# Carrying a hand-written instruction order two chunks into the second token block of a fused attention, feed-forward and routed-expert kernel

## The chip, the cores and the metric

The kernel runs on one core of a Trainium2 chip. The metric is the device time of one execution in microseconds (us); the median of three runs of the kernel before is 526.39 us (526.16 to 527.29). TensorE is called PE, VectorE DVE, ScalarE ACT, GpSimd POOL, and SyncE, which issues most of the loads, SP.

## What is computed

Three layers in a row, all in float32. The first is attention with a narrow local window plus one summary key per 32 positions (the maximum of the keys, the mean of the values):

```python
k_sum = k.reshape(B, H, nb, block, D).max(axis=3)
v_sum = v.reshape(B, H, nb, block, D).mean(axis=3)
scores_l = scale * np.matmul(q, k.transpose(0, 1, 3, 2))
...
scores_all = np.concatenate([scores_l_m, scores_s], axis=-1)
scores_all = scores_all - np.max(scores_all, axis=-1, keepdims=True)
a = np.exp(scores_all)
a = a / (np.sum(a, axis=-1, keepdims=True) + 1e-09)
```

with B=2, H=8, S=768, D=64. The second is a feed-forward layer on 1536 tokens of 512 values, with 2048 hidden units and an ELU between its two products. The third routes each token to one of 8 experts by the argmax of a gate, and each expert is a two-product ReLU layer (512 to 1024 to 512) whose result is scaled by two gate factors.

## The kernel before

The tokens go in four blocks, numbered 0 to 3, of 512, 256, 384 and 384 tokens (`UNITS` counts units of 64 tokens: 8, 4, 6, 6). Units 0 to 11 belong to the first batch entry, 12 to 23 to the second. For a unit u the attention runs scores (PE, line 330), maximum (DVE, line 340), exponential (ACT, line 353), normalising (DVE or POOL, line 401), transposing (PE, line 412), copying out of PSUM (ACT, line 419), product with the values (PE, line 449), and the split of the result into a high and a low part, xh (ACT, line 455) and xl (DVE, line 462), which are the inputs of the feed-forward layer. From block 1 on two units are a pair and share PSUM banks S and T.

The feed-forward layer goes through 16 chunks c of 128 hidden units for each block j. Below, h(j,c) is the first product (line 482, twelve matmuls, three for each of four slices, since each operand is a high and a low part), U its two exponent functions on ACT (line 495), V the two DVE steps that finish the ELU (lines 502 and 508; the second reads h out of PSUM and thereby frees its bank), g the split of the result (ACT line 518, DVE line 524), w the split of the second weight (ACT line 175, DVE line 179), and y(j,c) the second product (line 543). h has two PSUM banks, so h(j,c) cannot start before V of the chunk two earlier is done. During block 0 the weights are also unpacked and split (lines 130 to 167), which happens once. When y of a block is complete, it is copied out (lines 555 and 557), stored, transposed and turned into the gate's logits (line 579 on).

The summary keys and values of the second batch entry are reduced on DVE from loads of their own: eight reductions of keys, K (line 227), and eight of values, F (line 239). The copy of the F results into another layout, `pad`, is four DMAs on SP (`vsums2`, line 246), and three DVE copies take it into the value tiles (`v_pad`, line 255). Units 12 and 13 need the K results for their scores and `pad` for their product.

The order up to the transition from block 0 to block 1 is written out by hand in the table `START` of some 620 entries: `start_up` (line 717) walks it, and every engine gets its instructions in that order. An entry is a letter for the step and the numbers of unit, or chunk: `s9` scores of unit 9, `Gf` h of chunk 15, `Yd` y of chunk 13, `o`, `h`, `l` the product, xh and xl. Behind `START` a loop over (block, chunk) takes over, in which only PE has a written order, and a list scheduler at build time places the instructions of the other engines. In before, the loop begins at h(1,0), with y(0,14) and y(0,15) still to do. Each engine executes its instructions in the order in which they were built.

Routing constants (`route_consts`, line 758) are one load of 202 KB and some 14 small POOL instructions. In before they belong to the loop's part, and the scheduler puts them where it finds room.

Of the kernel before, what the change touches and what calls it, by code (L numbers as in the profile page):

```python
# [13 lines left out]
U32 = mybir.dt.uint32  # L14
# [8 lines left out]
E, F2 = 8, 1024  # L23
# [17 lines left out]
QS = (0, 2, 6, 8)  # L41
C3 = 2
WARM = 56
BITS = (0, 1, 2, 3, 6, 8)
PAIRS = {12: 35, 14: 45, 16: 54, 18: 65, 20: 74, 22: 83}
AT = (2, 6, 8, 8)
LQ = 5
# [34 lines left out]
class Prog:  # L82
# [42 lines left out]
    def conv_r(self, c, part):  # L125
# [13 lines left out]
    def conv_t(self, c, part):  # L139
# [112 lines left out]
    def v_pad(self, u):  # L252
# [363 lines left out]
    def part1(self):  # L616
# [22 lines left out]
        steps = [(j, c) for j in range(NBLK) for c in range(NF)]  # L639
        todo = {}  # L640

        def at(hs, fn, *args):
            todo.setdefault(hs, []).append((fn, args))

        for j in range(2, NBLK):
            for n in range(UNITS[j]):
                u = U0[j] + n
                h0 = PAIRS[u - n % 2]
# [28 lines left out]
        h0 = 2 * NF * (NBLK - 1)  # L677
# [39 lines left out]
    def start_up(self):  # L717

        unit = dict(k=self.k_sum, s=self.scores, m=self.maxes, b=self.less_max, e=self.weights, z=self.sums, r=self.recip, R=self.recip2, n=self.norm, t=self.turn_of, c=self.turned,
                    o=self.weighted, h=self.x_hi, l=self.x_lo, p=self.v_pad, x=self.max_k0, w=self.window, a=self.add_eps, M=self.mean_v0, P=self.pad_v0, K=self.red_sum, F=self.mean_v1, Z=self.keep_warm)  # L720
        load = dict(k=self.load_k0, Q=self.load_q0, V=self.load_v0, W=self.load_kw, c=self.load_c, w=self.load_w, q=self.load_q, v=self.load_v, s=self.load_sum, u=self.load_v1)
        part = dict(A=self.conv_r, B=self.conv_t, C=self.conv_f, D=self.conv_h, E=self.conv_l)
        chunk = dict(U=self.elu_act, V=self.elu_dve, Y=self.mm_y, g=self.g_high, f=self.g_low, i=self.w_high, j=self.w_low)
        half = set()
        for u in range(NV):
            self.unit0(u)
        with self.tc.manual_schedule():
            for op in START.split():
# [838 lines left out]
```

## Time and profile before

| what | value |
|---|---|
| median of 3 runs | 526.39 us |
| the profiled execution's own time | 526.98 us |
| its span, first to last instruction | 525.2 us |
| PE busy | 511.6 us (97%) |
| DVE busy | 337.1 us (64%) |
| ACT busy | 305.1 us (58%) |
| POOL busy | 54.4 us (10%) |

The busy shares are averages over very different stages: the attention of block 0 (to about 41 us), the rest of block 0 (to about 126 us), blocks 1 to 3, and the experts. PE's busy time counts modelled ends of matmuls, so gaps between matmul starts say more than the share does.

### The profile page before, as it was taken

The numbers are of one execution on the slowest core, as the hardware profiler recorded it, in microseconds if no ns is written. First come the engines' busy times: TensorE is split into PE (matmuls) and PEld (weight loads), VectorE is DVE, ScalarE is ACT, GpSimd is POOL, SyncE is SP. The second block draws the span as 40 slices with busy tenths as digits, with TensorE's granted clock in tenths as the row PEclk, the third lists the DMA queues.
The fourth block names the chain that finished last, engine by engine and source line by source line (L and its number), as shares of the span: only waits on it lengthen the run. The fifth ranks groups of instructions, "written<-read, shape, count | busy, mean of one in ns | idle before, by whom it ended". The sixth has DMA issues, their size and how long they took to land. (4 is left out here: it accounts for less than half of the span.)

```text
span 525.2 us, 9833 instructions
## 1 busy us (share of the span) xinstructions
PE 511.6 (97%) x3325; PEld 409.6 (78%) x3325; DVE 337.1 (64%) x945; ACT 305.1 (58%) x715; POOL 54.4 (10%) x102
## 2 busy tenths in 40 slices
PE   9999999998999999999999999999999999999994
PEld 6486778886888889888898897987888567576883
DVE  5899999997688868676557899668321011535410
ACT  3899998994677658656546547543232223656421
POOL 3530000001000000000000000113411111100001
PEclk9999999999999999999999999999999999999998
DMA  8999334551311212200001025310689898594601
GB/s 293 405 396 331 119 118 140 179 195 50 132 32 52 81 45 78 82 0 16 2 0 62 1 75 192 96 61 1 183 319 302 297 360 317 174 344 149 203 22 43
DMA packets 37131, 78.08 MB, mean 149 GB/s; under 512 B 3951, under 2 KB 9807, under 8 KB 37072
## 3 DMA queue, kind: packets, MB, share of 16 engines
q1 hardware_dynamic: 34752, 70.02, 39.2%
q0 software_dynamic: 2320, 7.34, 4.0%
q8 instruction: 28, 0.46, 0.4%
q14 instruction: 31, 0.25, 0.2%
HBM read 100.37 MB, written 6.55 MB: 204 GB/s over the span
## 5 line engine op out<-in xcount | busy, mean ns | idle before, releaser
L482 PE MATMUL h<-xh,wi 128*128 128x384 f32 (+2 forms) x528 | 142.8, 338 | 2.5 <-DVE elp L508 1.5
L543 PE MATMUL y<-wsp,gh 128*128 128x512 f32 x368 | 117.3, 400 | 0.0
L482 PEld LDWEIGHTS h<-xh,wi 128*128 128x128 f32 x528 | 94.5, 190 | 10.7 <-DVE elp L508 2.4
L482 PE MATMUL h<-xl,wi 128*128 128x384 f32 (+2 forms) x264 | 87.9, 333 | 1.6 <-DVE xl L462 1.6
L543 PEld LDWEIGHTS y<-wsp,gh 128*128 128x128 f32 x368 | 66.8, 190 | 12.3 <-issue 0.5
L543 PE MATMUL y<-wsp,gl 128*128 128x512 f32 x184 | 72.5, 394 | 0.0
L1222 DVE TENSOR_TENSOR holdl<-S,holdh 128x512 fp32r<-128x512 f32 x22 | 15.2, 690 | 72.5 <-ACT holdh L1218 53.7
L1190 PE MATMUL h<-w2s,holdh 128*128 128x512 f32 x176 | 59.8, 400 | 0.0
L1233 PE MATMUL y<-w2s,holdh 128*128 128x512 f32 x176 | 59.0, 398 | 0.0
L482 PEld LDWEIGHTS h<-xl,wi 128*128 128x128 f32 x264 | 50.2, 190 | 5.6 <-DVE xl L462 1.8
L502 DVE SCALAR_TENSOR_TENSOR elt<-ele,elt 128x384 f32<-128x384 f32 (+2 forms) x64 | 35.5, 554 | 24.6 <-ACT ele L495 24.3
L495 ACT ACTIVATE elt<-h 128x384 f32<-128x384 f32 (+2 forms) x64 | 31.2, 487 | 31.1 <-PE h L482 30.5
L175 ACT CAST wsp<-wo 128x512 fp32r<-128x512 f32 x62 | 38.0, 617 | 16.8 <-PE y L543 16.0
L179 DVE TENSOR_TENSOR wsp<-wo,wsp 128x512 fp32r<-128x512 f32 x62 | 42.6, 689 | 6.3 <-ACT wsp L175 6.0
L518 ACT CAST gh<-elp 128x384 fp32r<-128x384 f32 (+2 forms) x62 | 31.5, 508 | 23.5 <-DVE elp L508 12.8
L524 DVE TENSOR_TENSOR gl<-elp,gh 128x384 fp32r<-128x384 f32 (+2 forms) x62 | 34.0, 549 | 12.2 <-ACT gh L518 11.9
L543 PEld LDWEIGHTS y<-wsp,gl 128*128 128x128 f32 x184 | 34.7, 188 | 8.0 <-DVE gl L524 0.3
L353 ACT ACTIVATE e<-e,nb 128x120 f32<-128x120 f32 x88 | 33.6, 385 | 10.8 <-DVE nb L340 10.8
L1233 PEld LDWEIGHTS y<-w2s,holdh 128*128 128x128 f32 x176 | 33.1, 188 | 8.4 <-issue 1.6
L1190 PEld LDWEIGHTS h<-w2s,holdh 128*128 128x128 f32 x176 | 33.1, 188 | 8.2 <-ACT w2s L1258 0.8
L1264 DVE TENSOR_TENSOR w2s<-wo,w2s 128x512 fp32r<-128x512 f32 x48 | 30.8, 687 | 9.3 <-ACT w2s L1258 7.8
L508 DVE SCALAR_TENSOR_TENSOR elp<-elt,h 128x384 f32<-128x384 f32 (+2 forms) x64 | 35.1, 548 | 0.9
(290 smaller groups left out, 819.8 us busy)
## 6 DMA issues: line engine op xcount, KB each, us to landing
wo<-in_w SPq DMA_DIRECT2D x9, 2048.0 KB
wo<-in_w SPq DMA_DIRECT2D x18, 1024.0 KB
ri<-in_w_in SPq DMA_DIRECT2D x16, 512.0 KB
ro<-in_w_out SPq DMA_DIRECT2D x16, 512.0 KB
wo<-in_w SPq DMA_DIRECT2D x32, 256.0 KB
w2p<-in_w SPq DMA_DIRECT2D x32, 256.0 KB
w2q<-in_w SPq DMA_DIRECT2D x24, 256.0 KB
k<-in_kw SPq DMA_DIRECT2D x18, 192.0 KB
```

The costliest lines, as they stand in the source:

```text
L175: self.nc.scalar.copy(w[:, 0], self.w[c, 1].bitcast(F32))
L179: self.nc.vector.tensor_tensor(w[:, 1], self.w[c, 1].bitcast(F32), w[:, 0].bitcast(F32), op=ALU.subtract)
L353: nc.scalar.activation(e[:, p], e[:, p], AF.Exp, bias=nb[:, p:p + 1], scale=-1.0, accum_out=sm[:, p:p + 1])
L482: nc.tensor.matmul(h, lhsT=w[:, wl, k * 128:k * 128 + 128], rhs=x[:, k, a:b], start=(n == 0), stop=(n == 11))
L495: self.nc.scalar.activation(self.te[j, c][i], self.h[j, c], AF.Exp if i else AF.Tanh, scale=1.0 if i else 0.5)
L502: nc.vector.scalar_tensor_tensor(t, e, 1.0, t, op0=ALU.add, op1=ALU.mult)
L508: nc.vector.scalar_tensor_tensor(p, t, 0.0, h, op0=ALU.min, op1=ALU.max)
L518: self.nc.scalar.copy(gh, p)
L524: self.nc.vector.tensor_tensor(gl, p, gh.bitcast(F32), op=ALU.subtract)
L543: nc.tensor.matmul(self.y[j][t], lhsT=gx[:, sl], rhs=wx, start=(c == 0 and n == 0), stop=(c == NF - 1 and n == len(ops) - 1))
L1190: nc.tensor.matmul(self.h[s, hf], lhsT=x[:, k], rhs=w, start=(n == 0), stop=(n == 11))
L1233: nc.tensor.matmul(self.y2[s], lhsT=g[:, ks], rhs=w, start=(i == 0 and n == 0), stop=(i == 7 and n == 2))
```

## The change

The changed kernel walks a new `START`, which goes on through y(0,14), y(0,15), h(1,0), h(1,1) and the copying out of block 0's y (`FIXED = 2` chunks of block 1 belong to the table now, and the loop begins at h(1,2), after running what was planned for the half-steps of the two fixed chunks). The numbers in the table are read in base 36, so that `Gg` and `Gh` are chunks 0 and 1 of block 1. An entry `X` places the routing constants, and `O` copies out y. The table's entries are also in another order from the first load on, and some steps change their engine: `less_max` of units 3 and 4 from POOL to DVE, normalising of units 0, 1, 4 (instead of 3 and 6) on POOL, more copies of pad on ACT, one more weight addition on POOL, and one chunk fewer is unpacked in the way that `BITS` selects (one DVE instruction less, one ACT instruction more).

```diff
-BITS = (0, 1, 2, 3, 6, 8)
+BITS = (0, 1, 2, 3, 12)
...
-WE = "APPPPA"
-KE = "PVVVVPPP"
+WE = "AAPPPP"
+KE = "VPVPVAPP"
...
-EXP = (3, 4)
-NE = "VVVPVVPV"
-RADD = (0, 2, 3, 4, 6)
-PADA = (3,)
-CP = ((0, 0),)
+EXP = ()
+NE = "PPVVPVVV"
+RADD = (2, 3, 4, 5, 6, 7)
+PADA = (1, 4, 6)
+CP = ((1, 0), (3, 0))
...
+FIXED = 2
...
-        at(2 * NF, self.route_consts)
...
-            for i in range(NF, len(steps)):
+            for hs in range(2 * NF, 2 * NF + 2 * FIXED):
+                run(hs)
+            for i in range(NF + FIXED, len(steps)):
                 run(2 * i)
                 j, c = steps[i]
-                if c == 0 and 1 <= j < NBLK - 1:
+                if c == 0 and 2 <= j < NBLK - 1:
                     self.new_x(j + 1)
                 self.mm_h(j, c)
                 self.split_w(j, c)
-                if i > NF:
+                if i >= NF + FIXED:
                     self.split_g(*steps[i - 1])
...
-                n = [int(i, 16) for i in op[2 if k == "L" else 1:]]
+                n = [int(i, 36) for i in op[2 if k == "L" else 1:]]
...
+                elif k == "X":
+                    self.route_consts()
+                elif k == "O":
+                    self.out_y1(0, *n)
...
-                    self.mm_h(0, *n, TB // 2 if n[0] in half else 0)
+                    if n[0] == NF:
+                        self.new_x(2)
+                    self.mm_h(n[0] // NF, n[0] % NF, TB // 2 if n[0] in half else 0)
                 elif k in chunk:
-                    chunk[k](0, *n)
+                    chunk[k](n[0] // NF, n[0] % NF, *n[1:])
```

The table itself ends in this way, before and in the changed kernel:

```text
... oa cb ge F3 Be1 Vf1 Yd Ce1 ie ob Vf2 fe je jf gf ha F4 ff la
... ob ha Cf1 fe Yd Vf1 la ie Gg Lu7 if je Ls10 Vf2 Ls31 ih K10 F6 Ye F0 Ug1 ig gf
    Lu1 jf ff Ls30 Ug2 Vg1 Vg2 gg F1 Yf Gh K31 jh O0 fg Lu2 jg O1 F7 K30 O2 O3 F2 Uh1 Uh2 Vh1 Vh2
```

On PE, before, the last product of block 1's attention (tile S, values v) stands directly ahead of h(1,0), whose first two matmuls read xh and xl of block 1:

```order
L543 MATMUL y<-wsp,gh 128x512 x2
L543 MATMUL y<-wsp,gl 128x512
L449 MATMUL S<-et,v_100 64x64 x8
L482 MATMUL h<-xh_167,wi_545 128x256
L482 MATMUL h<-xl_168,wi_545 128x256
```

On PE, in the changed kernel, the same place (y_802 to y_805 are block 0's four y banks, h_1727 is h(1,0)):

```order
L450 MATMUL S_1620<-et_1595,v2_100 64x64 x8
L544 MATMUL y_802<-wsp_1656,gh_1652 128x512 x2
L544 MATMUL y_802<-wsp_1656,gl_1677 128x512
L544 MATMUL y_803<-wsp_1656,gh_1652 128x512 x2
L544 MATMUL y_803<-wsp_1656,gl_1677 128x512
L544 MATMUL y_804<-wsp_1656,gh_1652 128x512 x2
L544 MATMUL y_804<-wsp_1656,gl_1677 128x512
L544 MATMUL y_805<-wsp_1656,gh_1652 128x512 x2
L544 MATMUL y_805<-wsp_1656,gl_1677 128x512
L483 MATMUL h_1727<-xh1_167,wi0_397 128x256
L483 MATMUL h_1727<-xl1_168,wi0_397 128x256
```

The twelve matmuls of y(0,13) moved between the product and h(1,0). Behind h(1,0) the changed kernel has y(0,14), y(0,15), h(1,1), the scores of units 12 and 13, h(1,2), y(1,0), four transposes, h(1,3), y(1,1) and h(1,4); before has y(0,14), h(1,1), the scores, y(0,15), h(1,2) and from there on the same. PE has the same matmuls in both kernels, and from block 1's first chunks on every engine has the same order in both.

On DVE, before, the last F reduction (into vs), the weight split, xl of block 1, the three v_pad copies, and V of h(1,0):

```order
L239 TENSOR_REDUCE vs<-vn_1660 96x16
...
L179 TENSOR_TENSOR wsp<-wo,wsp 128x512
L462 TENSOR_TENSOR xl_168<-S,xh_167 128x4x128
L255 TENSOR_SCALAR v_98<-pad 24x512
L255 TENSOR_SCALAR v_99<-pad 24x512
L255 TENSOR_SCALAR v_100<-pad 24x512
L502 SCALAR_TENSOR_TENSOR elt<-ele,elt 128x256
L508 SCALAR_TENSOR_TENSOR elp<-elt,h 128x256
```

On DVE, in the changed kernel, from the last F reduction to the second V step of h(1,2) (the ISA rows on S and T are the maxima of units 12 and 13, half of them on each bank; the first elt is V of h(1,1), the last elt and elp are V of h(1,2)):

```order
L240 TENSOR_REDUCE vs<-vn_1821 96x16
L503 SCALAR_TENSOR_TENSOR elt<-ele,elt 128x256
...
L341 ISA e,nb<-S,mask 128x120
...
L256 TENSOR_SCALAR v_98<-pad 24x512
...
L341 ISA e,nb<-T,mask 128x120
...
L378 TENSOR_SCALAR r_1927<-s_1891 128x8
L379 RECIPROCAL r_1927<-r_1927 128x8
L402 TENSOR_TENSOR e<-e,r_1927 128x480 x2
L503 SCALAR_TENSOR_TENSOR elt<-ele,elt 128x256
L180 TENSOR_TENSOR wsp<-wo,wsp 128x512
L593 TENSOR_TENSOR mr<-y,mab 128x512
L509 SCALAR_TENSOR_TENSOR elp<-elt,h 128x256
```

The v_pad copies moved from a place ahead of all of block 1's V steps to a place between two halves of the maxima of units 12 and 13, with V of h(1,2) behind them, and the last F reduction moved from ahead of xl to behind the copying out of block 0's y. Ahead of the first row shown, between xl and this F, DVE now has the V steps of h(0,15) and h(1,0), the splits of y(0,14), y(0,15) and y(1,0), the four F reductions before it and three of the K reductions.

On POOL, early in the first block, before has the routing constants (rc, wg, tri, val) among the steps of the attention:

```order
L363 TENSOR_TENSOR e<-e,nb 128x480
L202 COPY k<-k_169 128x96
L385 TENSOR_SCALAR rr<-sm 128x4
L771 CAST wg_1743<-rc 128x4x16
L777 CAST tri<-rc 128x128
...
L385 TENSOR_SCALAR rr<-sm 128x4 x2
L774 TENSOR_TENSOR r_wg_1745<-r_wg_1745,wg_1743 128x64
L771 CAST wg_1743<-r_wg_1745 128x4x16
L401 TENSOR_TENSOR e<-e,rr 128x480
```

In the changed kernel all POOL instructions on rc stand behind the whole of block 0's attention, and their load is the 64th on SP instead of the 19th. The last row shown, the normalising of unit 3, is on DVE now.

## Rows read from the trace of the kernel before

**Rows 1.** Who PE waited for: line, releaser, us in total, times, longest.
```profile
PE h L482 <- DVE xl L462: 1.6, 1, 1.6
PE h L482 <- DVE elp L508: 1.5, 3, 0.7
PE T L412 <- POOL e L401: 1.1, 1, 1.1
...
PE h L482 <- ACT xh L455: 0.9, 1, 0.9
```

**Rows 2.** Three stretches: length, busy time (instructions) by engine, granted clock, DMA share, GB/s.
```profile
9.89:41.48 31.59, 29.38 (x396) 19.92 (x395) 28.46 (x118) 27.12 (x84) 13.35 (x30) 1.00 1.04 394
41.48:125.90 84.42, 84.42 (x440) 65.81 (x440) 82.32 (x182) 77.08 (x159) 1.32 (x2) 1.00 0.52 166
125.90:146.00 20.10, 17.61 (x125) 15.32 (x121) 13.30 (x41) 10.52 (x35) 0.82 (x2) 0.92 0.30 99
```

**Rows 3.** The same view, a stretch behind the transition.
```profile
128.85:132.65 3.80, 3.79 (x15) 3.51 (x16) 1.69 (x5) 0.66 (x2) 0.00 (x0) 0.55 0.03 8
```

**Rows 4.** PE in order of time: start, us, instruction, idle before it and releaser.
```profile
126.86 0.38 PE L482 MATMUL h<-xh,wi 128*128 128x256 f32 x1 [0.87 <-ACT xh L455]
128.85 0.39 PE L482 MATMUL h<-xl,wi 128*128 128x256 f32 x1 [1.61 <-DVE xl L462]
...
134.56 0.28 PE L482 MATMUL h<-xh,wi 128*128 128x256 f32 x1
...
137.06 0.73 PE L543 MATMUL y<-wsp,gh 128*128 128x512 f32 x2
...
139.91 0.28 PE L482 MATMUL h<-xh,wi 128*128 128x256 f32 x1
...
141.34 0.63 PE L543 MATMUL y<-wsp,gh 128*128 128x512 f32 x2
...
146.00 0.28 PE L482 MATMUL h<-xh,wi 128*128 128x256 f32 x1
```

**Rows 5.** DVE in order of time around the same place.
```profile
125.72 0.68 DVE L239 TENSOR_REDUCE vs<-vn 96x16 f32<-96x512 f32 x1
126.31 0.68 DVE L179 TENSOR_TENSOR wsp<-wo,wsp 128x512 fp32r<-128x512 f32 x1
...
128.12 0.68 DVE L462 TENSOR_TENSOR xl<-S,xh 128x512 fp32r<-128x512 f32 x1
130.92 1.08 DVE L255 TENSOR_SCALAR v<-pad 24x512 f32<-24x512 f32 x3 [2.12 <-DMA pad<-vs]
132.01 0.43 DVE L502 SCALAR_TENSOR_TENSOR elt<-ele,elt 128x256 f32<-128x256 f32 x1
```

**Rows 6.** The tile pad, its DMA issues: ns min/median/max, first and last start.
```profile
L246 SPq DMA_DIRECT2D pad<-vs x4: 713/726/919, 126.4 to 129.0; - x4
```

**Rows 7.** DVE in order of time, attention of units 12 and 13.
```profile
137.67 0.28 DVE L340 CUSTOM_DVE_ANT_0 e<-S,mask 128x120 f32<-128x120 f32 x1
...
141.64 0.17 DVE L377 TENSOR_SCALAR r<-s 128x8 f32<-128x8 f32 x1 [1.67 <-ACT e L353]
...
143.23 0.42 DVE L524 TENSOR_TENSOR gl<-elp,gh 128x256 fp32r<-128x256 f32 x1
```

**Rows 8.** ACT in order of time, the same place.
```profile
137.99 0.39 ACT L353 ACTIVATE e<-e,nb 128x120 f32<-128x120 f32 x1 [1.15 <-DVE nb L340]
...
139.14 0.58 ACT L557 ACTIVATE m<-y 128x512 f32<-128x512 f32 x1
...
142.77 0.61 ACT L175 CAST wsp<-wo 128x512 fp32r<-128x512 f32 x1
```

**Rows 9.** All engines in order of time, in block 0's attention.
```profile
22.34 0.34 POOL L771 CAST wg<-rc 128x64 bf16<-128x64 f32 x1 [3.54 <-DMA rc<-in_rc]
...
24.49 0.18 DVE L391 RECIPROCAL rr<-rr 128x4 f32<-128x4 f32 x1 [1.10 <-POOL rr L385]
...
25.54 0.98 POOL L401 TENSOR_TENSOR e<-e,rr 128x480 f32<-128x480 f32 x1
26.58 0.65 PE L412 MATMUL T<-c,e 128*120 128x128 f32 x4 [1.06 <-POOL e L401]
```

More of the change, by code (lines that the diff above doesn't have):

```diff
@@ L54 @@
 LG = ((6, 3, 4), (6, 4, 3), (5, 2, 2))
-WE = "APPPPA"
-KE = "PVVVVPPP"
+WE = "AAPPPP"
+KE = "VPVPVAPP"
 EXD = (3, 4)
-EXP = (3, 4)
-NE = "VVVPVVPV"
-RADD = (0, 2, 3, 4, 6)
-PADA = (3,)
-CP = ((0, 0),)
-START = "Lk2 Lk0 w02 Lk3 w43 Lk1 w13 x2 w42 w11 Lc0 x0 x3 w03 w20 w12 w23 w10 w50 x1 w30 w51 w53 LQ0 LQ1 Lc1 LV4 LV1 w01 w00 LW7 w22 k5 k3 w52 k1 k2 s0 s1 w21 k4 m0 s2 w32 s5 m1 m5 k0 w33 LV0 w40 m2 LW6 w41 e0 w31 M7 e1 s3 e5 s4 LV2 Lw00 m4 M2 LV3 LQ2 Lw10 M3 M0 a0 M1 e2 r0 m3 n0 t0 c0 r1 M5 M4 b4 M6 Lwd0 k7 b3 r5 k6 n1 t1 Lw01 a2 Lw30 e4 B00 n5 e3 A00 z4 P r2 c1 A10 s6 s7 z3 n2 a3 t5 p1 p0 p2 o0 c5 Lw50 r3 t2 B10 m6 p3 a4 r4 Lw51 h0 n3 l0 c2 o1 Z2 t3 e6 m7 p4 n4 c3 C00 Lq9 a6 o2 h1 Z8 o3 h2 D0 r6 Lw20 n6 h3 t4 C10 l2 Lwe0 o5 c4 l1 e7 Lw40 l3 E0 p7 t6 h5 Lw11 Lq8 B30 k8 H0 k9 r7 n7 c6 D1 p6 o4 A20 Lwf0 B20 t7 c7 o6 E1 h4 o7 C20 A30 Lw21 l5 l4 h6 h7 l6 Lw60 l7 B01 Lwa0 H1 D2 C30 G0 G1 A01 E2 C01 Lva Lw80 D3 U01 p8 Lv9 U02 E3 V01 V02 A11 B21 A21 B11 Ls00 C11 s8 C21 s9 U11 B51 B40 U12 Lqb i2 V11 A40 m8 A51 Lv8 V12 kb C40 G2 U21 Y0 Lw70 K00 Lqa D4 m9 U22 Lw31 C51 A50 B50 V21 Lwc0 A60 E4 G3 e8 V22 Y1 C50 A31 g2 j2 D5 B60 B31 C60 f2 Lw41 C31 U31 D6 E5 U32 B41 V31 ka Lw61 Ls11 E6 V32 i3 B70 A41 G4 C41 A70 K11 j3 U41 g3 U42 Y2 Lw71 G5 e9 A80 B80 V41 f3 V42 i5 U51 C70 g4 Y3 D7 R8 C80 n9 B61 Ls20 Lw90 D8 E7 E8 U52 Lwb0 V51 n8 G6 t8 A61 V52 Ba0 Aa0 U61 t9 C61 Ls01 i4 Ca0 U62 g5 c8 f4 Da G7 K20 V61 A90 j4 K01 i6 V62 c9 j5 B90 j6 f5 o8 Y4 B71 U71 Lw81 U72 A71 g6 o9 C90 Ea Ab0 V71 f6 Bb0 C71 Cb0 B81 Y5 Ls31 G8 D9 A81 V72 Db h8 E9 g7 U81 C81 Lw91 i7 l8 Eb K31 Y6 j7 Lu0 Ad0 U82 Bd0 f7 i8 B91 G9 V81 Cd0 A91 V82 j8 F0 Lu1 C91 U91 Y7 U92 sa g8 Lu5 V91 Lwa1 Lwb1 Bc0 V92 Ac0 ma F1 Dd f8 Ga F5 sb Y8 g9 Gb Cc0 Ba1 Ls30 ea Ua1 i9 Ua2 mb Va1 Aa1 eb f9 j9 K30 Ed Ra Va2 Ab1 Dc Bb1 Ub1 Ca1 Cb1 Ub2 ga Ec Lwc1 Y9 Ae0 Lu7 ia Lu2 Be0 Vb1 Gc na Vb2 Ce0 Ac1 Uc1 F7 ja Uc2 Ls21 De gb Bc1 Gd fa Cc1 Af0 ib Vc1 Bf0 F2 Vc2 ic Ee K21 Ud1 Lwd1 Ud2 Ad1 Lvb fb Ya jb Ge Lwf1 ta Yb Cf0 Bd1 Df Vd1 Ls10 Cd1 Vd2 jc Ef gc Lwe1 Af1 Bf1 Gf fc Ue1 nb Yc tb ca Ue2 gd id Lu6 Cf1 Ve1 F6 Ve2 if Lu4 K10 jd Lu3 fd Ae1 Uf1 Uf2 oa cb ge F3 Be1 Vf1 Yd Ce1 ie ob Vf2 fe je jf gf ha F4 ff la"
@@ new lines @@
+EXP = ()
[3 more added lines that the diff above has]
+CP = ((1, 0), (3, 0))
+START = "Lk3 x3 w13 Lk0 w03 w30 w53 x0 w50 Lk2 Lk1 w12 w02 w22 LQ0 x2 w00 x1 w20 k4 w01 w11 w52 w23 Lc0 s0 k1 w10 k3 s1 w32 k2 w21 w33 LQ1 Z2 s2 LV4 w42 k0 m0 k5 w51 w40 m1 e0 Lc1 s5 LV1 LV2 w41 e1 m5 Lw00 m2 e5 w43 LW7 LV0 r0 A00 M7 s4 w31 LQ2 s3 M3 m4 LW6 LV3 n0 Lw01 e2 M4 Lw10 r1 M2 B00 m3 t0 c0 b4 b3 n1 M5 a5 k6 a2 r5 C00 M0 r2 Lw90 M1 e3 e4 k7 D0 n5 z3 M6 P t1 c1 n2 p1 z4 s7 a3 Lw20 p0 s6 t5 B10 o0 o1 A10 c5 p4 Lq9 t2 p3 r3 m6 Lw70 a4 r4 h0 h1 C10 n3 m7 c2 e6 n4 B01 p7 p2 Z8 t3 o5 l1 c3 t4 Lq8 a6 e7 Lw50 o2 r6 Lw11 c4 h2 l0 o3 k8 n6 h3 o4 E0 t6 h5 a7 D1 r7 l2 k9 l3 H0 Lw30 h4 c6 n7 A20 p6 t7 Lw60 c7 Lw40 o6 B20 Lw21 o7 E1 C20 s8 B30 s9 Lw51 Lqa Lwa0 A30 h6 h7 D2 l5 l4 l6 l7 A01 G0 C30 D3 U01 E2 Lw80 B11 U02 C01 E3 Ls00 Lwf0 H1 V01 G1 V02 A11 A21 B21 U11 U12 G2 C11 K00 B50 C21 Lw41 A40 Y0 A50 V11 B40 V12 U21 C40 Lqb D4 Lv9 i2 U22 C50 m9 ka e9 m8 G3 A51 V21 E4 e8 V22 A41 Y1 U31 B41 B51 j2 C41 g2 D5 Lw31 Lv8 C51 Lw61 f2 G4 B31 E5 Y2 A31 U32 C31 V31 V32 i3 A60 B60 g3 j3 C60 f3 U41 G5 D6 U42 B61 E6 Lwb0 Lw91 V41 R8 V42 Y3 B70 A61 A70 n8 Lwc0 U51 C70 U52 g4 Lva Ls20 G6 n9 i5 V51 t9 K20 V52 D7 E7 A90 t8 C61 B80 i4 j4 G7 f4 A80 c8 Y4 C80 j5 B90 U61 D8 p8 C90 Lw71 U62 g5 V61 D9 Ls01 f5 o8 V62 E8 Ab0 Lwd0 kb Lwe0 Bb0 K01 c9 Cb0 U71 Y5 i6 Aa0 G8 U72 Ba0 Lw81 j6 g6 Ca0 V71 f6 E9 A71 B71 o9 Db V72 h8 U81 Eb C71 Y6 B81 g7 U82 Bd0 l8 V81 i7 A81 G9 f7 j7 Lvb Da Y7 Ea C81 Lwa1 Ad0 A91 Cd0 V82 Ac0 Bc0 i8 g8 B91 sb Cc0 U91 j8 C91 f8 U92 V91 i9 Aa1 sa Ls21 Ga V92 Dc Ua1 Dd g9 mb ma Lwb1 Ed Ec Y8 Ua2 j9 f9 K21 Va1 Va2 ea X eb Ra Gb Lwd1 Ab1 Y9 Lwe1 Ba1 Gc Ub1 Ca1 Ub2 Bb1 nb ga Vb1 ia Vb2 na Ae0 Be0 ja Uc1 Uc2 Cb1 ta Ce0 ca fa Bf0 Vc1 Af0 Cf0 De ib Gd Ya Ad1 gb Vc2 Lu5 Ee gc Bd1 Ls11 Cd1 Ge fb Df Ud1 F5 Lwc1 jb Be1 tb Ae1 Ef cb Lwf1 K11 Ud2 Ce1 Bc1 Vd1 Vd2 Yb oa Ac1 Lu3 Cc1 Ue1 Gf fc gd ic id jc Lu0 Bf1 Yc Ue2 fd Af1 Ve1 Ve2 Lu4 F3 jd Lu6 Uf1 Uf2 ge F4 ob ha Cf1 fe Yd Vf1 la ie Gg Lu7 if je Ls10 Vf2 Ls31 ih K10 F6 Ye F0 Ug1 ig gf Lu1 jf ff Ls30 Ug2 Vg1 Vg2 gg F1 Yf Gh K31 jh O0 fg Lu2 jg O1 F7 K30 O2 O3 F2 Uh1 Uh2 Vh1 Vh2"
```

## The prediction

> **What bounds the kernel now.** I read the busy shares first (PE 97%), then PE's list of waits, then stretches around the waits it names. PE does the same matmuls in both kernels, and from block 1's first chunks on every engine has the same order in both; so the time moves only by the time that PE loses ahead of that point, and by what it loses just behind it. PE's waits are few [rows 1]: 1.6 us for xl and 0.9 us for xh, each in one piece, both at the transition from block 0 to block 1; 1.1 us in one piece for a normalising step on POOL, and shorter ones for V. By stretches [rows 2], PE has 31.59 - 29.38 = 2.2 us idle in block 0's attention (from 9.89 us, when the warm-up matmuls end) and none in the rest of block 0, where DVE is busy 82.3 of 84.4 us and just keeps up. The third stretch, from the last product of block 1's attention (125.90) to the start of h(1,4) (146.00), has idle PE and a mean granted clock of 0.92. [...]
>
> **What the transition costs now.** Undisturbed, the work of the third stretch takes: h(1,1) to h(1,4) as it ran, 146.00 - 134.56 = 11.44; h(1,0), as h(1,2), 141.34 - 139.91 = 1.43; y(0,14), as y(0,15), 139.91 - 137.06 = 2.85 [rows 4]. Together 15.7 us of the 20.1. So 4.4 us are lost: 2.5 us of waits and the rest the low clock (3.80 us at 0.55 lose 1.7). This is what the change can take away: y(0,13) now lies between the product and h(1,0), 2.85 us that cover xh (0.58, as the other copies out of PSUM [rows 8]), one V step and xl (0.60 and 0.68, from three instructions of DVE between 126.31 and 128.12 and xl's own time [rows 5]). Cover is left: 2.85 - 0.1 - 0.58 - 0.60 - 0.68 = 0.9 us. Term one: -4.4.
>
> **What comes in its place.** The reductions that stood ahead of xl now stand behind it, the last F behind the copying out of block 0's y; and pad's four DMAs wait for that F, the three v_pad copies for pad, and behind them DVE has the second half of the maxima, the normalising of units 12 and 13, and V of h(1,2). h(1,4) needs the bank that this V frees, so PE is held there. I put the end of y(0,15) at 0.
>
> PE reaches h(1,4) undisturbed after h(1,1) and the scores (137.06 - 134.56 = 2.50) and everything from h(1,2) on (146.00 - 139.91 = 6.09 [rows 4]): at 8.6.
>
> DVE: xl ends 0.9 before h(1,0) starts, and h(1,0) starts 1.43 + 2 x 2.85 = 7.1 before 0: so at -8.0. From there to the end of the last F stand 9 instructions on 512 columns at 0.60, 5 F at 0.59 (126.31 - 125.72), 3 K at not more than 0.60, and 3 on 256 columns at not more than 0.43 [rows 5]: 11.4 together, which ends at +3.4. From the other side, one of these weight splits waits for a buffer that y(0,15) frees, and on ACT for the last copy of y: 0.58 + 0.61 on ACT [rows 8], then 0.68 on DVE and 0.68 for F [rows 5], so F cannot end before +2.5. I take 3.2, nearer to the count.
>
> From F's end on: pad's DMAs until v_pad may start, 130.92 - 126.40 = 4.5 [rows 5] (the four issues alone stretch over 126.4 to 129.0 plus 0.7 [rows 6]); the copies 1.1 (132.01 - 130.92); a maximum and four exponentials, 0.28 + 4 x 0.39 = 1.9 [rows 7, 8]; from the reciprocal's input to the end of the normalising 143.23 - 141.64 = 1.6 [rows 7]; then V's first step, a weight split, the logits' remainder and V's second step, 2 x 0.43 + 2 x 0.60 = 2.0. The sum is 11.1, so h(1,4) may start at 3.2 + 11.1 = 14.3 (13.6 with F at its earliest), 5.7 us (5.0) late. About one of these microseconds is lost already at the scores of unit 12, which need the last K, two places ahead of F, and a POOL copy. Term two: +5.7.
>
> The clock: in before it fell right behind 2.5 us of waiting. The new gap is longer, so I expect it to fall again; as part of the low stretch may lie inside the gap, I take 1.2 of the 1.9 that is not waiting in before, with 0 and 1.9 as ends. Term three: +1.2.
>
> That the wait is passed on hangs on DVE's keeping its order. In before DVE idled 2.12 us ahead of v_pad [rows 5], but there nothing behind it was ready much earlier, so this row does not show ready work being held. [...]
>
> **The start.** Of the 2.2 us that PE idles in block 0's attention [rows 2] one wait is 1.06 us at 26.58, for the normalising of unit 3 on POOL, which started at 25.54 [rows 9]; POOL had begun the routing constants at 22.34 after waiting for their load, and DVE waited 1.10 us for a step queued among them. The change takes the constants and their 202 KB away from there, and gives this normalising to DVE. What is late next: the transposes share one bank, ACT empties it, and ACT now has the four exponentials of unit 6 (4 x 0.39 [rows 8]) ahead of the copy that frees it for unit 4, so part comes back. Ahead of the first scores stand the same bytes (four key loads, mask, queries), so their wait stays. I take -0.9; the ends are -2.2, no idle left, and +1.1, one more wait as long as the longest here.
>
> The other edits (engines of copies and normalising, one chunk less by `BITS`) move some 2 us of DVE work away and 2 us to ACT over 115 us. In the rest of block 0, ACT has 77.1 and DVE 82.3 of 84.4 us busy [rows 2], PE hides both: 0. If one of them fell behind, I would charge 1.0 us, about two instructions of it. The constants at their new place lie on POOL, which has 1.3 us of work in those 84 us: 0.
>
> **Sum.** -4.4 + 5.7 + 1.2 - 0.9 + 0 = +1.6 us. Against the profiled execution's own time, 526.98, that is 528.6; that execution is 0.6 above the median of the runs, so I give **528.0** against 526.39. With the ends of the terms that weigh (start and clock partly against each other) the likeliest case lies between 525.8 and 529.8.
>
> **Rivals.** (a) *pad is there in time.* DVE itself has about 2.5 us of work between the last F and v_pad (three steps on 256 columns, four maxima, a wait for ACT). If the copies land within 2.5 us of F's end, 2.0 us of term two go and perhaps the fall of the clock: +1.6 - 2.0 - 0 to 1.2, so -0.4 to -1.6, about 525.4. For it speaks that one issue takes only 0.7 us; against it, that the same four took 4.5 us on an almost idle DMA system (share 0.03 [rows 3]). (b) *The change does what its covering y(0,13) offers and nothing is held behind*: V of h(1,2) is not late, terms two and three vanish: -5.3, 521.1. It decides if h(1,4) finds its bank free at 8.6 after y(0,15), which needs 5.7 us out of the chain. Against it stands every row of that chain; for it, only that DVE might have run further ahead, for which the floor of 13.6 leaves no room. (c) *The new order of the first 125 us meets a further wait*, with the clock falling once more: DVE and ACT have little slack there, and 1.1 + 1.7 us (the longest wait of the start, one low stretch [rows 3]) come on top: +4.4, 530.8. No view of before can show it.
>
> **How the numbers follow.** My forecast has 0.56, (a) 0.16, (b) 0.10, (c) 0.18. 0.2% is 1.05 us, about what can be told from no change. Slower by more than that: (c) and 0.40 of the forecast's 0.56, together 0.58. Within it: 0.13 of the forecast and half of (a), 0.21. Faster: (b), the other half of (a) and a remnant of the forecast, 0.21. The range leaves out most of (b) and the upper end of (c): 523.6 to 530.8.
>
> **What would show it.** Right: no wait for xl or xh at h(1,0); a wait of 4 to 5 us of PE at h(1,4), four chunks into block 1, put down to DVE's V step, with DVE idle ahead of v_pad until pad has landed and the clock low behind it; a wait of about 1 us ahead of the scores of unit 12, put down to POOL; the 1.06 us at unit 3's transposes gone. Wrong: v_pad that doesn't wait, h(1,4) that follows y(1,1) at once, or waits of PE between 41 and 126 us.

## The result, and the profile after

The changed kernel is slower: 534.48 us median of four runs (532.53 to 536.92) against 526.67, a ratio of 1.015 (95% interval 1.0101 to 1.0198). On a second chip it was 533.44 against 527.47, 1.0094 (1.0062 to 1.0125). The profiled execution took 532.53 us, 5.6 more than the one of before; its span is 530.8.

PE's waits in the changed kernel, in the view of [rows 1] (line, releaser, us in total, times, longest):

```profile
PE h L483 <- DVE elp L509: 5.7, 4, 4.2
PE S L331 <- POOL k L306: 2.3, 1, 2.3
PE T L188 <- DVE z L185: 1.1, 1, 1.1
PE h L483 <- ACT xh L456: 0.6, 1, 0.6
PE T L413 <- POOL rr L386: 0.6, 1, 0.6
PE h L483 <- DVE xl L463: 0.4, 1, 0.4
```

The two waits at the transition for xl and xh are gone (what stands there for them now is at the first h of block 0). In their place are 2.3 us at the scores of unit 12 and 4.2 us in one piece at an h. PE in order of time shows which:

```profile
126.40 0.28 PE L483 MATMUL h<-xh,wi 128*128 128x256 f32 x1
...
137.23 0.31 PE L331 MATMUL S<-k,q 64*64 64x120 f32 x1 [2.31 <-POOL k L306]
...
144.15 0.39 PE L544 MATMUL y<-wsp,gl 128*128 128x512 f32 x1
148.72 0.39 PE L483 MATMUL h<-xh,wi 128*128 128x256 f32 x1 [4.18 <-DVE elp L509]
```

The first row is h(1,0), which follows y(0,13) at once; the last is h(1,4), held until DVE's second V step of h(1,2) has read its bank. DVE in order of time says why that step is late:

```profile
127.84 0.55 DVE L228 TENSOR_REDUCE ks<-kst 128x12 f32<-128x384 f32 x1 [1.28 <-DMA kst<-in_kT]
...
135.87 0.54 DVE L228 TENSOR_REDUCE ks<-kst 128x12 f32<-128x384 f32 x1
...
136.93 0.67 DVE L240 TENSOR_REDUCE vs<-vn 96x16 f32<-96x512 f32 x1
137.53 0.41 DVE L503 SCALAR_TENSOR_TENSOR elt<-ele,elt 128x256 f32<-128x256 f32 x1
...
142.15 1.09 DVE L256 TENSOR_SCALAR v<-pad 24x512 f32<-24x512 f32 x3 [2.05 <-DMA pad<-vs]
143.17 0.26 DVE L341 CUSTOM_DVE_ANT_0 e<-T,mask 128x120 f32<-128x120 f32 x1
...
145.13 0.17 DVE L378 TENSOR_SCALAR r<-s 128x8 f32<-128x8 f32 x1 [1.08 <-ACT e L354]
...
148.26 0.41 DVE L509 SCALAR_TENSOR_TENSOR elp<-elt,h 128x256 f32<-128x256 f32 x1
```

The last reduction of values ends at 137.53; pad is there 4.6 us later; the second half of the maxima, whose scores had been in T since about 138.3, starts only behind the copies of pad; and the V step that h(1,4) needs ends at 148.7. The first row is a wait that the prediction did not have: the reduction K(1,0) waits 1.28 us for its load.

The same execution by stretches, in the columns of [rows 2]:

```profile
9.89:41.48 31.59, 29.37 (x396) 20.09 (x396) 27.76 (x115) 27.55 (x85) 13.78 (x26) 1.00 1.01 376
...
126.40:148.72 22.32, 15.83 (x121) 13.58 (x119) 17.24 (x49) 11.10 (x34) 1.00 (x4) 1.00 0.37 121
149.80:153.30 3.50, 3.50 (x19) 3.50 (x18) 1.61 (x4) 1.96 (x7) 0.00 (x0) 0.51 0.00 0
349.85:353.88 4.03, 4.03 (x38) 3.92 (x36) 1.07 (x2) 1.66 (x3) 1.43 (x3) 1.00 0.53 196
354.60:358.10 3.50, 3.50 (x12) 2.45 (x12) 1.93 (x13) 0.43 (x2) 0.00 (x0) 0.51 0.00 0
```

h(1,0) to h(1,4) takes 22.32 us, with PE busy for 15.83 (before, from the same point, 20.10 [rows 2]). Behind it the granted clock was 0.51 over 3.50 us, which costs 1.7. A second such stretch, at 354.6, has no counterpart in the profile of before; it follows on 4.03 us of small products, the last block's transposes and logits, in which PE never waits.

The account for the two profiled executions: h(1,0) could start at 126.40 instead of 125.90, +0.5; the stretch to h(1,4), +2.2; the clock behind it, +1.7; the later stretch of low clock, +1.7. That is 6.1 against 5.6 measured; the other 0.5 comes back in smaller pieces. The other runs of the changed kernel had granted clocks of 0.984 to 0.991 on average instead of 0.992, which fits the larger difference of the medians: 0.008 of 531 us is 4.2, and the slowest run took 4.4 more than the profiled one.

### The profile page after: what moved, and what is told of

Same layout as the page of the kernel before. It is cut to its first block, busy times and chain, and to the rows that moved or that the text cites. A ratio compares the mean times of both kernels' runs of the same rounds, so it can differ in the third digit from the quotient of the medians.

```text
span 530.8 us, 9826 instructions
## 1 busy us (share of the span) xinstructions
PE 512.8 (97%) x3325; PEld 410.9 (77%) x3325; DVE 336.9 (63%) x940; ACT 307.7 (58%) x719; POOL 55.8 (11%) x103
## 5 line engine op out<-in xcount | busy, mean ns | idle before, releaser
L1198 PE MATMUL h<-w2s,holdh 128*128 128x512 f32 x176 | 61.1, 408 | 0.0
L544 PEld LDWEIGHTS y<-wsp,gl 128*128 128x128 f32 x184 | 34.6, 188 | 8.0 <-DVE gl L525 0.5
```

The lines of the kernel that those rows point to most:

```text
L544: nc.tensor.matmul(self.y[j][t], lhsT=gx[:, sl], rhs=wx, start=(c == 0 and n == 0), stop=(c == NF - 1 and n == len(ops) - 1))
L1198: nc.tensor.matmul(self.h[s, hf], lhsT=x[:, k], rhs=w, start=(n == 0), stop=(n == 11))
```

## Experiments

The ratios are to the kernel before on the same chip, by 95% interval. For each run that bears on the transition I also give the time from the start of h(1,0) to that of h(1,4), which holds the same matmuls wherever y(0,13) stands ahead of h(1,0): 22.3 us in the changed kernel, 22.5 in its second profile.

**The changed kernel again.**

> The changed kernel once more, on the chip on which the next three run, so that they can be set beside it. The waits at the scores of unit 12 (2.3 us) and at h(1,4) (4.2 us) should stand again within 0.3 us if they follow from the order of the instructions; where the clock falls may differ. Ratio to before 1.010 to 1.015.

1.0094 (1.0062 to 1.0125), just below the range. Both waits stand as they were, 2.4 and 4.2 us: they follow from the order of the instructions. The two stretches of low clock are there too (granted 0.51 over 3.50 us from 150.5 and from 355.3).

**A late load's wait filled.**

```diff
-... Vf2 Ls31 ih K10 F6 Ye F0 Ug1 ...
+... Vf2 Ls31 ih F6 F0 Ye K10 Ug1 ...
```

> The changed kernel with one entry of its table moved: the key reduction whose load comes late stands behind two value reductions whose loads have long landed, instead of ahead of them. Theory: in the changed kernel DVE idles 1.28 us for that load, and everything behind it on DVE is late by as much; the predicted sum did not have this. Then DVE's idle time there falls to 0 to 0.2 us, PE's wait at the scores of unit 12 falls from 2.3 to about 1.0 us, the wait at h(1,4) stays near 4.2 us, and the time is about 1.3 us below the changed kernel's: 533.2 against 534.5. Rival (DVE's amount of work alone makes the scores late, the load's wait is covered): both waits stay, 534.5.

1.0111 (1.0079 to 1.0142). The wait for the load is gone, but DVE then waits 0.56 us for ACT, so everything behind is earlier by 0.7, not 1.3: the wait at the scores is 1.74 us, that at h(1,4) 4.17; h(1,0) to h(1,4) takes 21.7. The clock was low for longer in this execution (granted 0.51 from 145.7 to 152.5 us, 0.988 on average against 0.992), so that h(1,5) starts only 0.2 earlier than in the changed kernel. The trace shows the mechanism at half its size; the medians are too close to show it.

**The copies of pad on POOL.**

```diff
-            self.nc.vector.tensor_scalar(t[:NB], self.pad[:NB], 1.0 / 32.0, ...)
+            self.nc.gpsimd.tensor_scalar(t[:NB], self.pad[:NB], 1.0 / 32.0, ...)
```

> The changed kernel with the three copies of pad on POOL instead of DVE, all else in its table as it is. Theory: DVE keeps its order, so the copies, which wait 2.05 us for pad and take 1.1 us, hold the second half of the maxima and V of h(1,2) behind them. Without them on DVE the second half follows the first, about 3.1 us earlier, and PE's wait at h(1,4) falls from 4.2 to about 1.1 us: 531.4 against 534.5 for the changed kernel, or 1.7 us less again if the clock does not fall. The wait at the scores of unit 12 stays at 2.3. Rival (the exponentials or the late K results set V, not the wait for pad): the wait at h(1,4) stays above 3 us and the time within 1 us of 534.5.

1.0034 (1.0010 to 1.0058). DVE and POOL in order of time:

```profile
139.97 0.28 DVE L341 CUSTOM_DVE_ANT_0 e<-T,mask 128x120 f32<-128x120 f32 x1
...
142.65 0.17 DVE L378 TENSOR_SCALAR r<-s 128x8 f32<-128x8 f32 x1 [1.79 <-ACT e L354]
```

```profile
142.16 5.06 POOL L256 TENSOR_SCALAR v<-pad 24x512 f32<-24x512 f32 x3 [3.91 <-DMA pad<-vs]
```

Pad lands when it did, but now POOL waits, and the second half of the maxima starts at 139.97 instead of 143.17, 3.2 us earlier. Then the exponentials on ACT are the next limit, and the wait at h(1,4) falls to 2.2 us, not to 1.1: 20.3 from h(1,0) to h(1,4), and no low clock behind it (the last 128x256 matmul of h(1,4) took 0.29 us, 0.42 in the changed kernel). So pad held ready work on DVE. The three copies take POOL 5.06 us against DVE's 1.09.

**y(0,13) as cover, alone, in the kernel before.**

```diff
-... F3 Be1 Vf1 Yd Ce1 ie ob Vf2 fe je jf gf ha F4 ff la
+... F3 Be1 Vf1 Ce1 ie ob Yd Vf2 fe je jf gf ha F4 ff la
```

> The kernel before with one entry moved: y(0,13) between the last product of block 1's attention and h(1,0); all reductions stay ahead of xl, and the loop still begins at h(1,0). Theory: this alone is the gain of the change. Of the 2.5 us that PE waits for xh and xl at least 2 vanish, no clock falls at the transition, and nothing new is late: 522.1 to 523 against 526.5. Rival (what is behind xl on DVE is late next, V of h(1,0) or the pad copies): PE waits 2 us or more at h(1,1) to h(1,4), the clock falls again, and the time is 525 to 527.

0.9976 (0.9958 to 0.9993), far from the 522.1 of the theory. PE still waits at h(1,0), 0.97 us for xh and 0.86 for xl, and the clock still falls (two matmuls of y took 1.06 us at 131.33 and 0.62 at 133.74). ACT and DVE in order of time:

```profile
126.28 0.62 ACT L518 CAST gh<-elp 128x512 fp32r<-128x512 f32 x1 [1.28 <-PE y L543]
126.81 0.58 ACT L455 CAST xh<-S 128x512 fp32r<-128x512 f32 x1
```

```profile
127.95 0.68 DVE L462 TENSOR_TENSOR xl<-S,xh 128x512 fp32r<-128x512 f32 x1
```

On ACT xh stands behind the split gh of chunk 15, and that waits for y(0,13), from whose products it takes a buffer: the cover delays what it is to cover. On DVE xl stands behind splits and the reduction F4. The place of y(0,13) alone does not take the waits away; the changed kernel also has ACT and DVE in another order there.

**The same, with xh and xl first.**

```diff
-... F3 Be1 Vf1 Yd Ce1 ie ob Vf2 fe je jf gf ha F4 ff la
+... F3 Be1 Vf1 Ce1 ie ob Yd ha Vf2 la fe je jf gf F4 ff
```

> The kernel before with y(0,13) between the last product and h(1,0), as in the run that moved it alone, and xh ahead of the last split on ACT, xl ahead of the splits and the last reduction on DVE. Theory after that run: y(0,13) covered nothing there because xh stood on ACT behind a split whose buffer y(0,13) itself frees, and xl on DVE behind 3.5 us of splits and a reduction. With both first, xl ends near 125.6 us, y(0,13) near 126.7, PE waits under 0.3 us at h(1,0), the clock does not fall, and 2 to 3.7 us are gained: 523 to 525 against 526.5 to 527.8. Rival (DVE's backlog only moves on, as in the changed kernel): PE waits 2 us or more at h(1,2) to h(1,4), and the time is that of before.

0.9920 (0.9890 to 0.9949), 523.39 against 527.47. xl starts at 124.76, h(1,0) at 126.19, and the stretch up to h(1,4), in the columns of [rows 2], is

```profile
126.19:141.81 15.62, 15.62 (x121) 13.73 (x120) 13.29 (x42) 10.46 (x34) 1.04 (x2) 1.00 0.34 114
```

without a wait or a low clock, which is the undisturbed 15.7 us of the prediction. Only one reduction, F4, stands behind xl here, where the changed kernel has eight; pad has landed before DVE comes to its copies.

**The routing constants in mid-block, in the kernel before.**

```diff
-        at(2 * NF, self.route_consts)
...
+                elif k == "X":
+                    self.route_consts()
...
-... Ls30 ea Ua1 ...
+... Ls30 ea X Ua1 ...
```

> The kernel before with the routing constants placed in its table behind the exponential of unit 10, all else as it is. Theory of the prediction: PE's wait of 1.06 us for the normalising of unit 3 on POOL comes from the constants ahead of it, so that wait goes and 0.5 to 1.0 us with it: about 525.7 against 526.5, with the transition as before. Rival (the wait only moves to the next step of the start, which DVE and ACT set): block 0's attention ends as late as before, 526.5.

0.9970 (0.9952 to 0.9989), 525.84 against 527.8. The 1.1 us of PE for POOL's normalising [rows 1] are no longer among the waits, and h(1,0) starts 0.7 us earlier, although PE lost 1.0 us more to the first load of queries in this profile. The wait went as forecast; the medians differ by more, 2.0 us.

**Both, and pad on POOL.** The edits of the last two and of the second experiment together.

> The same with the routing constants in mid-block and the three copies of pad on POOL. Theory: the normalising of unit 3 costs PE no wait (0.8 us), and DVE does not stand still for pad, so what may be late at h(1,2) to h(1,4) in the run without these is up to 2 us earlier: 521.5 to 524. Rival (pad and constants were covered): as the run without them.

0.9897 (0.9868 to 0.9926), 522.12 against 527.47: faster than both kernels. h(1,0) starts at 124.86 and h(1,4) 15.62 us later. The gain beyond the run without constants and POOL is about that of the constants alone; pad on POOL shows no gain of its own, since nothing waited there.

**The old head with the new transition.** The old table up to the last product, without the eight reductions that the changed kernel has behind it, with the constants in mid-block and the old engines; then the changed kernel's order.

```diff
-... Lu6 Cf1 Ve1 F6 Ve2 if Lu4 K10 jd Lu3 fd ... F3 Be1 Vf1 Yd Ce1 ie ob Vf2 fe ... la
+... Cf1 Ve1 Ve2 if Lu4 jd Lu3 Lu0 Lu6 fd ... F3 Be1 Vf1 Ce1 F4 ob ha fe Yd la ie Gg Lu7 ... Vh2
```

> The changed kernel's order from the last product on, with its eight late reductions, behind the old order and the old engines of the first 125 us (the constants in mid-block). It tells the first block's new order from the transition. Theory: the waits at the scores of unit 12 and at h(1,4) come from the transition's order and stay at 2 to 2.5 and 4 to 4.5 us, while y(0,13) ends 0.8 to 1.5 us earlier than the 126.4 us of the changed kernel, since the new order's own waits (xh and xl at the first h, a late unpacking) are gone: about 1 us below the changed kernel. Rival (the new order of the first 125 us is the main loss, and leaves DVE too far behind): the waits of the transition fall below 4 us together, and the time comes near that of before.

0.9962 (0.9944 to 0.9981), 525.55: some 8 us below the changed kernel on this chip, where 1 was expected. h(1,0) starts at 124.55, 1.9 us earlier. The waits behind it are smaller too:

```profile
134.73 0.31 PE L331 MATMUL S<-k,q 64*64 64x120 f32 x1 [1.69 <-POOL k L306]
...
143.21 0.39 PE L483 MATMUL h<-xh,wi 128*128 128x256 f32 x1 [1.15 <-DVE elp L509]
```

h(1,0) to h(1,4) takes 18.7 us, and no clock falls there (granted 1.00). Waits below 4 us together and a time near that of before are the rival's two signs, but its reason, a DVE that the new first order leaves too far behind, explains little of them. The last reduction of values ends 10.5 us behind the start of h(1,0) instead of 11.1, since the load of K(1,0) is in time here. The other 3 us are the list scheduler's: the table behind the product is the same, but the copies of pad stand behind all eight maxima this time, and the second V step directly behind the first. DVE in order of time:

```profile
134.47 0.68 DVE L240 TENSOR_REDUCE vs<-vn 96x16 f32<-96x512 f32 x1
...
139.70 1.09 DVE L256 TENSOR_SCALAR v<-pad 24x512 f32<-24x512 f32 x3 [1.24 <-DMA pad<-vs]
...
142.28 0.42 DVE L503 SCALAR_TENSOR_TENSOR elt<-ele,elt 128x256 f32<-128x256 f32 x1
142.73 0.42 DVE L509 SCALAR_TENSOR_TENSOR elp<-elt,h 128x256 f32<-128x256 f32 x1
```

**Cover at the first h.**

```diff
-... A30 h6 h7 D2 l5 l4 l6 l7 A01 G0 C30 ... E3 Ls00 Lwf0 H1 V01 G1 ...
+... A30 H1 h6 h7 D2 l5 l4 l6 l7 A01 G0 C30 ... E3 Ls00 Lwf0 V01 G1 ...
```

> The changed kernel with one entry moved in the first 125 us: the first half of h(0,1) ahead of the second half of h(0,0), where the kernel before has it. Theory: the new first order took this cover away, so PE waits for xh and xl of the last units of block 0's attention (0.64 + 0.38 us). With it back both waits fall to under 0.2 us, block 0 runs on 0.7 to 1.3 us earlier, and h(1,0) starts at 125.1 to 125.7 us instead of 126.4: 532.4 against 533.4 for the changed kernel on the second chip. Rival (the attention is late by its engines, not by the order on PE): PE waits as long one chunk later, h(1,0) at 126.4.

1.0063 (1.0038 to 1.0088). The rival is right on its subject: PE waits as long one chunk later (1.3 us, now for V), and h(1,0) starts at 126.23. But this edit of the first 40 us also changed the scheduler's choice 100 us later: the copies of pad stand behind all the maxima, the only move on DVE ahead of h(1,4). DVE in order of time:

```profile
140.44 0.28 DVE L341 CUSTOM_DVE_ANT_0 e<-T,mask 128x120 f32<-128x120 f32 x1
...
141.97 1.08 DVE L256 TENSOR_SCALAR v<-pad 24x512 f32<-24x512 f32 x3 [1.25 <-DMA pad<-vs]
142.99 0.15 DVE L378 TENSOR_SCALAR r<-s 128x8 f32<-128x8 f32 x1
...
146.10 0.41 DVE L509 SCALAR_TENSOR_TENSOR elp<-elt,h 128x256 f32<-128x256 f32 x1
```

The exponentials now run while DVE waits for pad, and V ends 2.2 us earlier than in the changed kernel: 20.3 us from h(1,0) to h(1,4), as with pad on POOL.

**Three edits together** (the first half of h(0,1) ahead, the late load's wait filled, pad on POOL).

> The changed kernel with three edits, each tried alone: the first half of h(0,1) back ahead, two value reductions ahead of the late key reduction, the copies of pad on POOL. If the account of the waits is whole they add up: 1.0 + 0.7 + 2.1 us off, the wait at h(1,4) near 2.2 and that at the scores near 1.7 us, and 1.7 us more if the clock does not fall behind h(1,4): 528 to 529.7 against 533.4. Rival (they share one backlog of DVE, so that what is gained early is waited for later): 531 or more.

1.0075 (1.0048 to 1.0101), 530.81, between the forecast (528 to 529.7) and the rival (531 or more). The waits are as forecast, 1.74 us at the scores and 2.15 at h(1,4). The first edit's 1.0 us did not come, as in its own run; h(1,0) starts at 126.83, with 1.0 us lost to the first load of queries, and the clock fell behind h(1,4) in the profiled execution (granted 0.991 on average, 0.994 with pad on POOL alone).

**The new engines under the old order** (the kernel before, the constants in mid-block, and the changed kernel's `BITS`, `WE`, `KE`, `EXP`, `NE`, `PADA`, `CP`).

> The kernel before with the constants in mid-block and, of the changed kernel, the engines of copies, normalising and unpacking (all its new assignments but those of one small addition), under the old order. It tells engines from order in the first 125 us, of which the run with the old head has shown that the changed kernel loses 1.9 us there. Theory: the assignments are the loss, since DVE and ACT share their work differently; then the last product of block 1's attention ends 0.8 us or more later than in the run that moved only the constants, and the time is 526.5 to 528. Rival: the order is the loss, and with the assignments alone the time stays within 0.7 us of the run with the constants alone (0.997 of before).

1.0016 (0.9998 to 1.0035), against 0.9970 with the constants alone: the assignments cost about 2.5 us under the old order, and h(1,0) starts 2.6 us later, as the theory has it (528.50 us, just above its range). New among PE's waits are

```profile
PE h L482 <- DVE wi L167: 1.2, 2, 1.0
...
PE y L330 <- DVE nb L340: 0.8, 1, 0.8
```

**The last keys earlier.**

```diff
-... K31 jh O0 fg Lu2 jg O1 F7 K30 O2 O3 F2 ...
+... K31 K30 jh O0 fg Lu2 jg O1 F7 O2 O3 F2 ...
```

> The changed kernel with its last key reduction ahead of the copying out of y and of one value reduction; the list scheduler then also places the pad copies behind all the maxima. Theory: the wait at the scores of unit 12 (2.3 us) goes, since POOL's copies start 3 us earlier, but h(1,4) still waits for the chain from the last value reduction over pad to V: it starts 20 us behind h(1,0) instead of 22.3, as in the run in which the pad copies alone stood behind the maxima, and PE waits there as much longer as the scores are earlier: 4 to 4.5 us. Time 2 us below the changed kernel: 531.4. Rival (the two waits are independent, and both gains add): h(1,4) starts 18 us behind h(1,0), the time is 529 or less.

1.0122 (1.0096 to 1.0148). The wait at the scores is gone, yet h(1,4) starts 22.3 us behind h(1,0), as in the changed kernel. PE, then SP's issues, in order of time:

```profile
142.79 0.73 PE L544 MATMUL y<-wsp,gh 128*128 128x512 f32 x2 [1.02 <-ACT gh L519]
146.76 0.80 PE L544 MATMUL y<-wsp,gl 128*128 128x512 f32 x1 [3.24 <-DVE gl L525]
149.24 0.58 PE L483 MATMUL h<-xh,wi 128*128 128x256 f32 x1 [0.40 <-DVE elp L509]
```

```profile
136.26 0.33 SPq L290 DMA_DIRECT2D k<-in_kw  x1
136.69 2.81 SPq L565 DMA_DIRECT2D mdram<-m  x3
139.56 0.45 SPq L292 DMA_DIRECT2D q<-in_q  x1
140.09 3.23 SPq L247 DMA_DIRECT2D pad<-vs  x4
```

The four transfers of pad are queued on SP behind a load of keys and queries that the scheduler moved ahead. SP waited 2.6 us for PE's scores before it issued the key load, one of the three stores queued behind that took 1.9 us to issue, and pad's transfers start 2.5 us later than in the changed kernel. The copies on DVE wait 2.70 us, and PE now waits for the split behind them, at y(1,1). The gain of 2 us that the theory expected went there. By the order of the changed kernel the wait at the scores should be no loss of its own, since V stands behind pad, which lands later anyway; as pad moved too, this run does not show it.

## Why the prediction was wrong

Direction and mechanism of the transition were right; the time fell outside the range, at 1.5% instead of 0.3%. The profiled execution took 5.6 us more where the sum had 1.6. By its own steps, the start and the other edits were 1.4 too low, the chain over pad 0.9 and the clock 0.5; a second fall of the clock, which the sum did not have, adds 1.7, and 0.5 comes back.

**The waits removed, -4.4: right.** h(1,0) follows y(0,13) at once. By the runs the cover and the new places of xh and xl are both needed, and the sum counted both. With y(0,13) moved alone, PE still waits 1.8 us at h(1,0). With xh and xl first as well, xl still ends 2.0 us behind the last product, and y(0,13) covers that. The new places without y(0,13) were not run.

**The chain over pad, +5.7: right in kind, 0.9 short.** PE waited 2.3 and 4.2 us, 6.5 together (6.6 from h(1,0) to h(1,4)). Pad took 4.6 us where the prediction had 4.5, and 11.2 us lie between the last F's end and V's end (137.53 to 148.7) where it had 11.1. What it missed is ahead of F: it counted DVE's work up to there without a wait, and took F's end at 3.2 behind y(0,15), that is 136.5; the load of K(1,0) cost 1.28, and F ended at 137.53. The run that fills this wait gives back 0.7 of it. That DVE holds ready work behind a waiting instruction, on which this term rests and of which the rows of before showed nothing, is now shown: the second half of the maxima ran at 139.97 with pad on POOL and at 143.17 behind it. How much the chain costs hangs on the scheduler's place for the copies: behind all the maxima it is 2.0 us less, with nothing else moved on DVE (the run with cover at the first h).

**The clock, +1.2: one fall as forecast, at 1.7, and a second not in the sum.** The fall at 354.6, another 1.7 us, follows on small products and not on a wait. Of the fourteen profiled executions here, seven have one at this place (granted 0.51 over 3.50 us in both of the changed kernel, 0.51 over 3.45 us with only the constants moved) and seven, with the same small products, have none (1.00 over the 3.50 us from 350.0 in before). The eight with the changed kernel's order behind the product have six of them; the six with the old order have one, with only the constants moved. What decides, and whether the new order makes it likelier, is open.

**The start, -0.9, and the other edits, 0: this step failed.** The wait of 1.06 us for POOL went, and the gain of the constants is real (0.3%, 1.6 us, by their own run), but the changed kernel's h(1,0) could start 0.5 us later than before: PE's waits up to there come to 2.5 us instead of 2.1. One of them lies between 41 and 126 us (0.43 at 59.96), which the prediction had named as a sign of being wrong. In place of the old wait stand others, and the first h waits for xh and xl:

```profile
28.18 0.62 PE L413 MATMUL T<-c,e 128*120 128x128 f32 x4 [0.57 <-POOL rr L386]
...
36.25 0.38 PE L483 MATMUL h<-xh,wi 128*128 128x256 f32 x1 [0.64 <-ACT xh L456]
37.02 0.39 PE L483 MATMUL h<-xl,wi 128*128 128x256 f32 x1 [0.38 <-DVE xl L463]
...
59.96 0.47 PE L483 MATMUL h<-xh,wi 128*128 128x512 f32 x1 [0.43 <-DVE elp L509]
```

ACT and DVE, in order of time, say why xh and xl are late. Each has an unpacking step ahead of them that waits for a load of the first product's weights, while the product that xh and xl split ends on PE at 34.6:

```profile
34.90 0.80 ACT L131 ACTIVATE cv_r<-ri 128x512 uint16<-128x512 uint32 x1 [1.00 <-DMA ri<-in_w_in]
35.57 0.63 ACT L456 CAST xh<-y 128x256 fp32r<-128x256 f32 x2
```

```profile
34.84 0.45 DVE L147 TENSOR_SCALAR cv_t<-ri 128x512 int32<-128x512 int32 x1 [1.31 <-DMA ri<-in_w_in]
...
35.55 1.41 DVE L463 TENSOR_TENSOR xl<-y,xh 128x256 fp32r<-128x256 f32 x4
```

In the kernel before and with the old head neither engine waits for a load there. With the new order and its first h in place, PE's wait for xh follows ACT's wait for the load: 0.64 us for 1.00, 0.7 for 1.12 (the last keys earlier), 0.4 for 0.79 (pad on POOL), 0.2 for 0.58 (the second profile), none for 0.45 (the late load's wait filled). So here, too, ready work stood behind an instruction that waited for a transfer.

"PE hides both: 0", said of the moved copies, normalising and unpacking, is what was wrong, and the 1.0 us charged to it at worst was too little: under the old order the same assignments cost about 2.5 us; with the new order around them the changed kernel is 1.9 behind the old head. The busy shares could not show it: in the first stretch of the changed kernel ACT and DVE are busy for 27.6 and 27.8 of 31.6 us, and the cost lies in what stands behind their waits. How the 1.9 us divide among the entries is open; the one tried, the first half of h(0,1), only moved a wait. Rival (c), a further wait in the first 125 us and one more fall of the clock, comes nearest to what happened, though both were there in part only.

## What to carry over

When an engine has no slack, moving its work behind an urgent step pays only as far as nobody waits for the moved work: find the last consumer of each, and the transfers between. Here a reordering of three or four entries on ACT and DVE, with one reduction moved, gave 4 us. Eight reductions moved cost 6.6 us behind the urgent step, or 3.0 where the copies of pad came to stand behind all the maxima and the late load was in time. An instruction that waits for a transfer, a copy or an unpacking step, belongs on an engine, or at a place, where nothing urgent stands behind it (here the wait for pad and its copies held half of the maxima for 3.2 us); and where a list scheduler fills in around a fixed table, read where such a copy has landed after every edit of the table, even one far ahead of it.

## What was unexpected of the hardware

A low clock that lies ahead of a wait cost nothing here: with the cover at the first h, the clock stood at 0.50 over the scores,

```profile
136.80:140.20 3.40, 3.15 (x38) 2.84 (x39) 2.90 (x16) 1.26 (x6) 0.94 (x4) 0.50 0.45 162
```

and PE then waited only 0.80 us at h(1,4) where it waits 2.15 us with pad on POOL, although V ends at the same time (146.5 and 146.6 us). And the clock does not fall alike in all executions of one kernel: before ranged from 524.8 to 530.7 us on the later chips, its mean granted clock from 0.990 to 0.997. What decides it is not shown here. The first wait for the queries' load varied as well, from under 0.2 to 1.6 us.
